# Attention and two MLPs on one core: conversions of weights moved behind a copy, and the last batch's scores, u and xT put in another order

## The chip, the core and the metric

One Trainium2 chip, one of its cores. The metric is the device time of one execution in microseconds (us), median of several executions; lower is better. The profile names the engines PE (matrix multiplies; PEld is its weight loads), DVE (vector), ACT (scalar), POOL and SP; SP issues most of the transfers (DMA).

## The reference

```python
def _attn_ref(q, k, v, phi):                       # all (4, 8, 576, ...), 32 memory slots
    a = softmax(phi, axis=2)                       # over the 32 slots of a token
    k_m = einsum('bhsm,bhsd->bhmd', a, k)          # 32 x 64 for each batch and head
    v_m = einsum('bhsm,bhsd->bhmd', a, v)
    attn = softmax(q @ k_m.T / 8, axis=-1)
    return attn @ v_m
x = attn_out as (2304, 512)
x = ((x @ w_a) * (x @ w_b)) @ w_out                # 512 -> 1536 -> 512
y = elu(x @ w_in) @ w_out2                         # 512 -> 2048 -> 512
```

As the kernel and its rows show it, phi's maximum and sum run over the 576 tokens of one slot (axis 2 of phi). q and k are drawn 200 times larger than v and phi.

## The kernel before

The weights come as 64-bit floats. A "unit" is one 128x512 block; it is loaded raw (512 KB, a POOL transfer) and turned into two float32r parts, high and low, by a fixed run of small steps on ACT (L113 magnitude, L119 low word, L133 the high part) and DVE (L155, L158, L142, L163, L168, L173, L176). `piece()` does the next step of the current unit, and `fill(n)` does n of them at the place where it is called. The step that begins a unit on DVE (L155) reads what ACT's L113 made for that unit.

All instructions are issued by hand: each engine runs its own instructions in the order in which the code calls them.

The first part of the kernel (to about 104 us) is the attention, one loop over the four batches i = 0 to 3. In iteration i, PE contracts a with k and v (`stage_kv`, L360), the means are turned (`stage_turn`, L380), PE makes the scores of batch i-1 (`stage_scores`, L401 and L405), and transposes a of batch i+1 (`stage_aT`, PE L336 and L338). ACT copies these transposes to SBUF (L340 and L343), which the next iteration's `stage_kv` reads. DVE makes the softmax of batch i-1 (`stage_softmax`: L427 maximum, L429 subtraction, ACT L431 exp) and, an iteration later, its sums and division (`stage_norm`: L445 to L451). `stage_xT` transposes the result on PE (L462, L466), rounds it into `xhi` on ACT (L69) and makes the rest `xlo` on DVE (L70).

attn @ v_m is never made. Instead u = v_m @ w is made for each 128 columns of w (`step_u`, PE L489, in two halves of 12 matmuls), rounded on ACT (L504), its rest made on DVE (L500), and spread by eight or sixteen small transfers into tiles `u` by batch (L513); the ab steps (`steps_ab`, PE L629) multiply u by xhi and xlo. The tile `ur`, in which u is rounded, has one buffer. For the first columns (f = 0), u is made for batches 0 and 1 in iteration 3 and for batches 2 and 3 behind the loop.

PSUM is held as two tiles of two banks (`pstile`, pool ps0) and four of one bank (`pone`, pool ps1); behind the attention ps1 is closed and its banks become two more of two banks (ps2). A step's deferred work (`defer`) runs in a later `step` or `tick`.

Order of the calls around the change, before:

```python
            stage_vT(i)
            if i:
                stage_scores(i - 1)
            fill(FILLS[i])
            if i + 1 < B:
                stage_aT(i + 1)
            if i:
                soft_tiles(i - 1)
                stage_softmax(i - 1)
```

Behind the loop: u of batches 2 and 3 (both halves), scores of batch 3, division and xT of batch 2, softmax and division of batch 3, then the ab steps of batches 0 and 1, u for the next columns, xT of batch 3, the ab steps of batch 2 and so on.

Of the kernel before, what the change touches and what calls it, by code (L numbers as in the profile page):

```python
# [7 lines left out]
F32 = mybir.dt.float32  # L8
# [5 lines left out]
AF = mybir.ActivationFunctionType  # L14
ALU = mybir.AluOpType
# [6 lines left out]
def attention_then_two_mlps(ctx, tc, q, kv, kv_left, phi, w_ab, w_o1, w_i2, w_o2, out):  # L22
# [13 lines left out]
    nc = tc.nc  # L36
    B, P, KC, S = q.shape
    M = 32
# [5 lines left out]
    SM = NJ * P  # L44
    LEFT = S - SM
# [15 lines left out]
    def pstile(name):  # L61
        turn[0] += 1
        return pss[turn[0] % len(pss)].tile([P, 2, 512], F32, tag="ps", name=name)

    def pone(name):
        return pstile(name)[:, 0] if len(pss) == 2 else ps1.tile([P, 512], F32, tag="one", name=name)

    def split_sb(hi, lo, src):
        nc.scalar.activation(out=hi, in_=src, func=AF.Copy)  # L69
        nc.vector.tensor_tensor(out=lo, in0=src, in1=hi.bitcast(F32), op=ALU.subtract)  # L70
# [117 lines left out]
    def drop(key):  # L188
        ready.pop(key)
        live[units[index[key]][1]] -= 1  # L190
# [3 lines left out]
    def fill(amount):  # L194
        credit[0] += amount
        while credit[0] >= 1.0:
            credit[0] -= 1.0
            if not piece():
                credit[0] = 0.0


    FILLS = 6, 6, 6, 6
# [35 lines left out]
    def tick():  # L238
        step(lambda: None, [], 0, "012")
# [11 lines left out]
    xhi = [pa.tile([P, 2, S], F32R, name=f"xhi{b}") for b in range(B)]  # L251
    xlo = [pa.tile([P, 2, S], F32R, name=f"xlo{b}") for b in range(B)]
# [75 lines left out]
    def stage_aT(b, us=(0, 1)):  # L328
        t = st["phi", b]
        if us[0] == 0:  # L330
            st["a", b] = p0.tile([P, 2, NJ + 1, P], F32, tag="a", name="a_t", bufs=1)
        a = st["a", b]
        tp, tl = pstile("tp_a"), pone("tl_a")
        for u in us:
            for j in range(NJ):
                nc.tensor.transpose(tp[:, u, j * P:(j + 1) * P], t[:, u, j * P:(j + 1) * P], ident)  # L336
        for u in us:
            nc.tensor.transpose(tl[0:LEFT, u * P:(u + 1) * P], t[:, u, SM:S], ident)  # L338
        c = slice(us[0], us[-1] + 1)
        nc.scalar.activation(  # L340
            out=a[:, c, 0:NJ, :].rearrange("p u j s -> p u (j s)"), in_=tp[:, c], func=AF.Copy
        )
        nc.scalar.activation(  # L343
            out=a[0:LEFT, c, NJ, :], in_=tl[0:LEFT, 0:2 * P].rearrange("p (u s) -> p u s", u=2)[:, c], func=AF.Copy
        )
        if us[-1] == 1:
            more_loads("phi")
# [46 lines left out]
    def stage_scores(b):  # L394
        qs = [st.pop(("q", b, u)) for u in range(2)]
        kt = kts[b % 2]
        sc, sl = pstile("sc"), pone("sl")
        for u in range(2):
            for j in range(NJ):
                for t in range(2):  # L400
                    nc.tensor.matmul(sc[:, u, j * P:(j + 1) * P], qs[u][:, t, j * P:(j + 1) * P],  # L401
                                     kt[:, u, t * P:(t + 1) * P], start=(t == 0), stop=(t == 1))
        for u in range(2):
            for t in range(2):
                nc.tensor.matmul(sl[0:LEFT, u * P:(u + 1) * P], qs[u][:, t, SM:S],  # L405
                                 kt[:, u, t * P:(t + 1) * P], start=(t == 0), stop=(t == 1))
        more_loads("q", "q")
        st["sc", b] = [
            (sc.rearrange("p u (g m) -> p u g m", m=M), P, 4 * NJ),
            (sl[0:LEFT, 0:2 * P].rearrange("p (u g m) -> p u g m", u=2, m=M), LEFT, 4),  # L410
        ]
# [38 lines left out]
            for o, m in both(at, n, sm):  # L450
                eng.tensor_tensor(out=o, in0=o, in1=m.to_broadcast(list(o.shape)), op=ALU.mult)  # L451

    def stage_xT(b):
        (at, _, _), (al, _, _) = st.pop(("at", b))
        tp, tl = pstile("tp_x"), pone("tl_x")

        def half(t, u):
            return t[u] if isinstance(t, list) else t[:, u]

        for u in range(2):  # L460
            for j in range(NJ):
                nc.tensor.transpose(tp[:, u, j * P:(j + 1) * P],  # L462
                                    half(at, u)[:, 4 * j:4 * j + 4, :].rearrange("p g m -> p (g m)"), st["ident"])
        split_sb(xhi[b][:, :, 0:SM], xlo[b][:, :, 0:SM], tp)
        for u in range(2):
            nc.tensor.transpose(tl[:, u * LEFT:(u + 1) * LEFT],  # L466
                                half(al, u)[0:LEFT].rearrange("p g m -> p (g m)"), st["ident"][0:LEFT, 0:LEFT])
        split_sb(xhi[b][:, :, SM:S], xlo[b][:, :, SM:S], tl[:, 0:2 * LEFT].rearrange("p (u s) -> p u s", u=2))

    u_t, g_t = {}, {}  # L470

    def step_u(f, amount, bs=tuple(range(B))):

        us = {b: pu.tile([P, 2, 2, 256], F32R, tag="u", name="u", bufs=5) for b in bs}
        ur = pu.tile([P, 2, KC, 2, 256], F32R, tag="ur", name="ur", bufs=1)
        u_t.update({(f, b): us[b] for b in bs})

        def half(k):  # L480
            ps = pstile("u_ps")

            def pe():
                whi, wlo = weights(("ab", f, k))
                for c in range(2):
                    for n, (v, w) in enumerate(((vthi, whi), (vthi, wlo), (vtlo, whi))):
                        for i in range(2):
                            r = slice(64 * i, 64 * i + 64)
                            nc.tensor.matmul(  # L489
                                ps[:, i, c * 256:c * 256 + 256], v[r, 2 * k + c].rearrange("p b m -> p (b m)"),  # L490
                                w[r, c * 256:c * 256 + 256], start=(n == 0), stop=(n == 2),
                            )
                if bs[-1] == B - 1:
                    drop(("ab", f, k))

            src = ps.rearrange("p i (c n) -> p i c n", c=2)
            hi, lo = [ur[:, :, 2 * k:2 * k + 2, x] for x in range(2)]

            def lower():
                nc.vector.tensor_tensor(out=lo, in0=src, in1=hi.bitcast(F32), op=ALU.subtract)  # L500
                if k == 1:
                    spread()

            step(pe, lambda: nc.scalar.activation(out=hi, in_=src, func=AF.Copy), amount / 2)  # L504
            defer(1, lower)

        def spread():
            for b in bs:
                for c in range(2):
                    for i in range(2):  # L510
                        o = 64 * c + M * i
                        src = ur[M * b:M * b + M, i].rearrange("p (k c) h n -> p k c (h n)", c=2)[:, :, c ^ (b % 2)]
                        nc.sync.dma_start(out=us[b][o:o + M].rearrange("p k h n -> p k (h n)").bitcast(F32),  # L513
                                          in_=src.bitcast(F32))

        half(0)
        half(1)

    with tc.manual_schedule():
        make_identity(nc, ident)  # L520
# [21 lines left out]
        for i in range(B):  # L542

            for n in (1, 0):
                for u in range(2):
                    stage_kv(i, n, u)
                stage_m(i, n)
            if i == 0:
                fill(4)
                a_max(1, 0)  # L550
                a_max(1, 1)
                a_exp(1, 0)
                a_exp(1, 1)
            if i > 1:
                stage_norm(i - 2, nc.vector)
            if i + 1 < B:
                a_end(i + 1, 0)
                a_end(i + 1, 1)
            if i == B - 1:
                step_u(0, 0, (0, 1))  # L560
            tick()
            if i > 1:
                stage_xT(i - 2)
            stage_turn(i, 1)
            stage_turn(i, 0)
            stage_kT(i)
            stage_vT(i)
            if i:
                stage_scores(i - 1)
            fill(FILLS[i])  # L570
            if i + 1 < B:
                stage_aT(i + 1)
            if i:
                soft_tiles(i - 1)
                stage_softmax(i - 1)
            if i + 2 < B:
                a_max(i + 2, 0)
                a_max(i + 2, 1)
                a_exp(i + 2, 0)
                a_exp(i + 2, 1)  # L580
        step_u(0, 0, (2, 3))
        tick()
        stage_scores(B - 1)
        stage_norm(B - 2, nc.vector)
        stage_xT(B - 2)


        last = B - 1
# [17 lines left out]
        st["at", last] = [(ats, *[rest[:, k, :, 0:4 * NJ] for k in range(2)]),  # L606
                          (als, *[rest[:, k, :, 4 * NJ:] for k in range(2)])]
        stage_softmax(last)
        tick()
        es_p.close()  # L610
        pss.append(ctx.enter_context(tc.tile_pool(name="ps2", bufs=2, space=PSUM, reuse_waits="tile")))
        stage_norm(last, nc.vector)
        tick()

        def steps_ab(f, b, amount):
            u = u_t.pop((f, b))
# [279 lines left out]
```

## Time and profile before

| | us |
|---|---|
| median of 3 runs (837.27 to 840.36) | 837.71 |
| the profiled execution | 838.2 |
| its span in the profile | 836.4 |
| PE busy in it | 794.7 (95%) |
| DVE busy | 610.3 (73%) |
| ACT busy | 413.6 (49%) |

The profile is one execution. The span is the time from its first to its last instruction; about 1.8 us of the execution's own time lie outside it. Shares of busy time are means over stages of different limits. PEclk is the share of TensorE's full clock that was granted.

### The profile page before, as it was taken

The numbers are of one execution on the slowest core, as the hardware profiler recorded it, in microseconds if no ns is written. First come the engines' busy times: TensorE is split into PE (matmuls) and PEld (weight loads), VectorE is DVE, ScalarE is ACT, GpSimd is POOL, SyncE is SP. The second block draws the span as 40 slices with busy tenths as digits, with TensorE's granted clock in tenths as the row PEclk, the third lists the DMA queues.
The fourth block names the chain that finished last, engine by engine and source line by source line (L and its number), as shares of the span: only waits on it lengthen the run. The fifth ranks groups of instructions, "written<-read, shape, count | busy, mean of one in ns | idle before, by whom it ended". The sixth has DMA issues, their size and how long they took to land.

```text
span 836.4 us, 13805 instructions
## 1 busy us (share of the span) xinstructions
PE 794.7 (95%) x5576; PEld 739.7 (88%) x5576; DVE 610.3 (73%) x1015; ACT 413.6 (49%) x636; POOL 43.1 (5%) x91
## 2 busy tenths in 40 slices
PE   4686799999999999999999999999999999999998
PEld 3575789999999999999999898889998889998896
DVE  4497877878887888567788852887777876776555
ACT  4354456655454444334358753566554565543360
POOL 3000000000000000000000000000000000000000
PEclk9598899999999999999999999999999999999999
DMA  9973267664775277516001200111111110100006
GB/s 302 367 252 91 61 161 178 159 152 109 176 175 125 80 177 177 125 30 150 26 1 51 74 27 1 53 49 52 50 51 51 51 51 25 51 26 1 1 1 226
DMA packets 32175, 82.95 MB, mean 99 GB/s; under 512 B 4848, under 2 KB 4848, under 8 KB 32112
## 3 DMA queue, kind: packets, MB, share of 16 engines
q1 hardware_dynamic: 22320, 46.41, 20.5%
q0 software_dynamic: 9792, 35.66, 14.4%
q8 instruction: 44, 0.72, 0.4%
q14 instruction: 19, 0.16, 0.1%
HBM read 52.17 MB, written 4.72 MB: 68 GB/s over the span
## 4 chain that ended last, share of the span: by engine, by line
PE 87%; DVE 4%; DMA 4%; ACT 2%; issue 1%; SPq 1%; POOL 1%; DVEq 0%; ACTq 0%; POOLq 0%
PE o_ps L796 24%; PE h_ps L753 24%; PE o_ps L671 17%; PE ab_ps L629 16%; DMA raw<-in_w_ab_dram 3%; PE u_ps L489 2%; PE sc L401 2%; PE pk L360 1%; DVE ur L500 1%; SPq L513 1%; DMA u<-ur 1%; DVE a_sb L638 0%; DVE at L429 0%; ACT gh L639 0%; DVE a L163 0%
## 5 line engine op out<-in xcount | busy, mean ns | idle before, releaser
L629 PE MATMUL ab_ps<-xhi,u 128*128 128x288 f32 x768 | 141.0, 301 | 5.3 <-DVE ur L500 2.6
L629 PEld LDWEIGHTS ab_ps<-xhi,u 128*128 128x128 f32 x768 | 116.1, 192 | 7.4 <-DVE ur L500 3.0
L796 PE MATMUL o_ps<-ulh,g2h 128*128 128x512 f32 x288 | 114.2, 397 | 0.0
L796 PE MATMUL o_ps<-ull,g2h 128*128 128x512 f32 x288 | 114.2, 396 | 0.0
L796 PE MATMUL o_ps<-ulh,g2l 128*128 128x512 f32 x288 | 103.5, 397 | 0.0
L771 DVE SCALAR_TENSOR_TENSOR e<-e,th 128x768 f32<-128x768 f32 x48 | 46.0, 959 | 76.5 <-ACT e L768 76.2
L753 PE MATMUL h_ps<-yh,usl 128*128 128x384 f32 x384 | 98.2, 336 | 0.0
L753 PE MATMUL h_ps<-yh,ush 128*128 128x384 f32 x384 | 98.1, 336 | 0.0
L753 PE MATMUL h_ps<-yl,ush 128*128 128x384 f32 x384 | 98.1, 336 | 0.0
L764 ACT ACTIVATE e<-h_ps 128x768 f32<-128x768 f32 x48 | 39.0, 812 | 96.1 <-PE h_ps L753 94.1
L629 PE MATMUL ab_ps<-xlo,u 128*128 128x288 f32 x384 | 83.3, 299 | 0.0
L671 PE MATMUL o_ps<-gh,ulh 128*128 128x288 f32 x384 | 83.0, 297 | 0.1
L671 PE MATMUL o_ps<-gh,ull 128*128 128x288 f32 x384 | 82.4, 296 | 0.0
L671 PE MATMUL o_ps<-gl,ulh 128*128 128x288 f32 x384 | 82.4, 295 | 0.0
L753 PEld LDWEIGHTS h_ps<-yh,ush 128*128 128x128 f32 x384 | 69.7, 188 | 1.3
L753 PEld LDWEIGHTS h_ps<-yh,usl 128*128 128x128 f32 x384 | 69.5, 188 | 0.0
L753 PEld LDWEIGHTS h_ps<-yl,ush 128*128 128x128 f32 x384 | 69.5, 188 | 0.0
L638 DVE TENSOR_TENSOR a_sb<-a_sb,ab_ps 128x576 f32<-128x576 f32 x48 | 36.1, 753 | 42.2 <-PE ab_ps L629 35.7
L796 PEld LDWEIGHTS o_ps<-ulh,g2l 128*128 128x128 f32 x288 | 54.2, 188 | 13.2
L796 PEld LDWEIGHTS o_ps<-ull,g2h 128*128 128x128 f32 x288 | 54.3, 188 | 12.5
L796 PEld LDWEIGHTS o_ps<-ulh,g2h 128*128 128x128 f32 x288 | 54.3, 188 | 12.5
L629 PEld LDWEIGHTS ab_ps<-xlo,u 128*128 128x128 f32 x384 | 63.0, 192 | 0.0
(115 smaller groups left out, 1385.2 us busy)
## 6 DMA issues: line engine op xcount, KB each, us to landing
u<-ur SPq DMA_DIRECT2D x192, 128.0 KB, 5.0
raw<-in_w_o_dram POOLq DMA_DIRECT2D x28, 512.0 KB, 4.1
raw<-in_w_ab_dram POOLq DMA_DIRECT2D x24, 512.0 KB, 5.6
kv_t<-in_kv_dram SPq DMA_DIRECT2D x16, 512.0 KB, 8.4
raw<-in_w_i_dram POOLq DMA_DIRECT2D x16, 512.0 KB, 3.7
q_t<-in_q_dram SPq DMA_DIRECT2D x8, 576.0 KB, 9.9
out_dram<-y SPq DMA_DIRECT2D x8, 512.0 KB, 2.9
phi_t<-in_phi_dram SPq DMA_DIRECT2D x3, 576.0 KB, 10.4
```

Source lines behind the costliest of these rows:

```text
L360: nc.tensor.matmul(pk[M * h:M * h + M, D * u:D * u + D], a[0:P if j < NJ else LEFT, u, j, M * h:M * h + M], rows, start=(j == 0), stop=(j ...
L401: nc.tensor.matmul(sc[:, u, j * P:(j + 1) * P], qs[u][:, t, j * P:(j + 1) * P], kt[:, u, t * P:(t + 1) * P], start=(t == 0), stop=(t == 1))
L489: nc.tensor.matmul(ps[:, i, c * 256:c * 256 + 256], v[r, 2 * k + c].rearrange("p b m -> p (b m)"), w[r, c * 256:c * 256 + 256], start=(n = ...
L500: nc.vector.tensor_tensor(out=lo, in0=src, in1=hi.bitcast(F32), op=ALU.subtract)
L513: nc.sync.dma_start(out=us[b][o:o + M].rearrange("p k h n -> p k (h n)").bitcast(F32), in_=src.bitcast(F32))
L629: nc.tensor.matmul(ps[:, h, 0:HS], u[:, kk, w, n * P:n * P + P], x[b][:, kk, h * HS:(h + 1) * HS], start=(kk == 0 and i == 0), stop=(kk == ...
L638: nc.vector.tensor_tensor(out=a_sb, in0=a_sb, in1=ps[:, :, 0:HS], op=ALU.mult)
L671: nc.tensor.matmul(ps[:, h, 0:HS], w[:, cc], g[:, h * HS:(h + 1) * HS], start=(n == 0 and i == 0), stop=(n == len(fs) - 1 and i == 2),)
L753: nc.tensor.matmul(ps[:, h, 0:HB], w[:, c], x[:, c, h * HB:(h + 1) * HB], start=(c == 0 and i == 0), stop=(c == KC - 1 and i == 2),)
L764: nc.scalar.activation(out=e, in_=ps[:, :, 0:HB], func=AF.Relu, scale=-1.0)
L771: nc.vector.scalar_tensor_tensor(out=e, in0=e, scalar=1.0, in1=th, op0=ALU.add, op1=ALU.mult)
L796: nc.tensor.matmul(ps[:, k, :], g[:, c * P:(c + 1) * P], w, start=(f == fs[0] and i == 0), stop=(f == fs[-1] and i == 2),)
```

## The change

Four edits. (1) In the loop, `fill` moves behind `stage_aT`, so that ACT's steps of the conversion are called behind its copies of the transposed a. (2) Behind the loop the scores of batch 3 come first; u of batches 2 and 3 is made in halves, the first half behind these scores, the second behind the softmax of batch 3 and behind the change of PSUM pools. (3) `step_u` rounds and subtracts only the partitions of its own batches (64 of 128 where it has two batches). (4) xT of batch 2 is held in three one-bank tiles instead of one of two banks and one of one; its rounding and subtraction are done by half, and the subtraction is called behind the softmax of batch 3.

```diff
-    def stage_xT(b):
+    def stage_xT(b, single=False):
         (at, _, _), (al, _, _) = st.pop(("at", b))
-        tp, tl = pstile("tp_x"), pone("tl_x")
+        if single:
+            tps, tl = [pone("tp_x") for _ in range(2)], pone("tl_x")
+        else:
+            tp, tl = pstile("tp_x"), pone("tl_x")
+            tps = [tp[:, u] for u in range(2)]
...
-        split_sb(xhi[b][:, :, 0:SM], xlo[b][:, :, 0:SM], tp)
...
-        split_sb(xhi[b][:, :, SM:S], xlo[b][:, :, SM:S], tl[:, 0:2 * LEFT].rearrange("p (u s) -> p u s", u=2))
+        parts = [(slice(SM, S), slice(0, 2), tl[:, 0:2 * LEFT].rearrange("p (u s) -> p u s", u=2))]
+        if single:
+            parts = [(slice(0, SM), u, tps[u]) for u in range(2)] + parts
+        else:
+            parts = [(slice(0, SM), slice(0, 2), tp)] + parts
+
+        def upper(c, u, src):
+            nc.scalar.activation(out=xhi[b][:, u, c], in_=src, func=AF.Copy)
+
+        def lower(c, u, src):
+            nc.vector.tensor_tensor(out=xlo[b][:, u, c], in0=src, in1=xhi[b][:, u, c].bitcast(F32), op=ALU.subtract)
+
+        if not single:
+            for p in parts:
+                upper(*p)
+                lower(*p)
+            return None
+        for p in parts:
+            upper(*p)
+        return lambda: [lower(*p) for p in parts]
...
-    def step_u(f, amount, bs=tuple(range(B))):
+    def halves_u(f, amount, bs=tuple(range(B))):
...
-            src = ps.rearrange("p i (c n) -> p i c n", c=2)
-            hi, lo = [ur[:, :, 2 * k:2 * k + 2, x] for x in range(2)]
+            r = slice(M * bs[0], M * bs[-1] + M)
+            src = ps[r].rearrange("p i (c n) -> p i c n", c=2)
+            hi, lo = [ur[r, :, 2 * k:2 * k + 2, x] for x in range(2)]
...
-        half(0)
-        half(1)
+        return [lambda: half(0), lambda: half(1)]
+
+    def step_u(f, amount, bs=tuple(range(B))):
+        for half in halves_u(f, amount, bs):
+            half()
...
             if i:
                 stage_scores(i - 1)
-            fill(FILLS[i])
             if i + 1 < B:
                 stage_aT(i + 1)
+            fill(FILLS[i])
...
-        step_u(0, 0, (2, 3))
+        stage_scores(B - 1)
+        halves = halves_u(0, 0, (2, 3))
+        halves[0]()
+        stage_norm(B - 2, nc.vector)
         tick()
-        stage_scores(B - 1)
-        stage_norm(B - 2, nc.vector)
-        stage_xT(B - 2)
+        lower_x = stage_xT(B - 2, True)
...
         stage_softmax(last)
-        tick()
+        lower_x()
         es_p.close()
         pss.append(ctx.enter_context(tc.tile_pool(name="ps2", bufs=2, space=PSUM, reuse_waits="tile")))
+        halves[1]()
+        tick()
         stage_norm(last, nc.vector)
-        tick()
```

## Rows read from the trace of the kernel before

**Rows 1.** Windows: stretch, its us, busy us (instructions) by engine, clock, DMA share, GB/s.
```profile
80.00:86.00 6.00, 6.00 (x40) 5.88 (x40) 4.39 (x9) 0.00 (x0) 0.00 (x0) 0.73 0.57 131
...
104.00:146.00 42.00, 39.67 (x288) 38.02 (x288) 32.52 (x57) 24.27 (x56) 3.22 (x6) 0.96 0.72 167
146.00:836.00 690.00, 686.05 (x4224) 643.01 (x4224) 507.67 (x818) 343.85 (x490) 30.29 (x55) 1.00 0.28 78
```
**Rows 2.** Timeline, iteration 0: start, us, instruction, [engine idle before, who ended it].
```profile
20.80 0.66 PE L336 MATMUL tp_a<-ident,phi_t 128*128 128x128 f32 x4 [0.16 <-DVE phi_t L321]
...
24.50 0.65 ACT L119 ACTIVATE lw<-raw 128x512 bf16<-128x512 uint32 x1 [2.29 <-DMA raw<-in_w_ab_dram]
25.06 1.00 ACT L340 ACTIVATE a_t<-tp_a 128x1024 f32<-128x1024 f32 x1
...
26.12 1.08 PE L360 MATMUL pk<-kv_t,a_t 128*32 128x64 f32 x32 [4.44 <-ACT a_t L340]
...
34.16 0.37 PE L360 MATMUL pk<-kv_t,a_t 128*32 128x64 f32 x2 [2.82 <-issue]
```
**Rows 3.** DMA queues between 31 and 35 us: packets, MB, share.
```profile
q8 instruction: 1, 0.02, 2.0%
```
**Rows 4.** Timeline, iteration 1 and the begin of 2.
```profile
37.07 0.68 ACT L113 ACTIVATE a<-raw 128x512 f32<-128x512 f32 x1
...
38.50 0.42 DVE L155 TENSOR_SCALAR a<-a 128x512 f32<-128x512 f32 x1
...
41.41 1.22 DVE L427 TENSOR_REDUCE smx<-sc 128x32 f32<-128x1024 f32 x1 [0.83 <-PE sc L401]
...
43.51 1.02 ACT L340 ACTIVATE a_t<-tp_a 128x1024 f32<-128x1024 f32 x1 [4.26 <-PE tp_a L336]
...
44.43 0.36 ACT L343 ACTIVATE a_t<-tl_a 64x256 f32<-64x256 f32 x1
...
49.39 1.06 PE L462 MATMUL tp_x<-ident,at 128*128 128x128 f32 x8 [1.42 <-DVE at L451]
```
**Rows 5.** Timeline, iterations 2 and 3.
```profile
54.61 0.42 DVE L155 TENSOR_SCALAR a<-a 128x512 f32<-128x512 f32 x1
...
56.01 1.22 DVE L427 TENSOR_REDUCE smx<-sc 128x32 f32<-128x1024 f32 x1
...
57.45 1.02 ACT L340 ACTIVATE a_t<-tp_a 128x1024 f32<-128x1024 f32 x1 [2.09 <-PE tp_a L336]
...
65.20 1.09 PE L462 MATMUL tp_x<-ident,at 128*128 128x128 f32 x8 [1.66 <-DVE ur L500]
```
**Rows 6.** Timeline behind the loop.
```profile
74.57 1.36 ACT L431 ACTIVATE at<-at 128x1024 f32<-128x1024 f32 x2 [2.65 <-DVE at L429]
...
77.46 1.94 ACT L504 ACTIVATE ur<-u_ps 128x1024 fp32r<-128x1024 f32 x2 [1.52 <-DMA u<-ur]
...
79.79 5.44 PE L401 MATMUL sc<-kt,q_t 128*128 128x128 f32 x32 [4.13 <-DVE ur L500]
80.79 1.53 DVE L445 TENSOR_REDUCE ssm<-at 128x32 f32<-128x1024 f32 x2
...
82.96 1.50 DVE L451 TENSOR_TENSOR at<-at,ssm 128x1024 f32<-128x1024 f32 x2
...
88.37 1.23 DVE L70 TENSOR_TENSOR xlo<-tp_x,xhi 128x1024 fp32r<-128x1024 f32 x1 [3.91 <-ACT xhi L69]
...
93.01 1.26 DVE L445 TENSOR_REDUCE small<-at 128x16 f32<-128x512 f32 x2
...
103.72 0.85 PE L629 MATMUL ab_ps<-xhi,u 128*128 128x288 f32 x2 [2.61 <-DVE ur L500]
```
**Rows 7.** Windows of u's matmuls alone (columns as in Rows 1, POOL left out).
```profile
72.00:74.00 2.00, 0.98 (x12) 0.78 (x12) 0.00 (x0) 0.00 (x0) 1.00 0.87 294
```
**Rows 8.** The tile ur: its spreading transfers, 66 to 135 us.
```profile
L513 SPq DMA_DIRECT2D u<-ur x39: 585/595/1621, 66.3 to 134.4; - x39
...
DMA to landing us min/median/max: 2.3/4.0/6.5
```

More of the change, by code (lines that the diff above doesn't have):

```diff
@@ L461, in stage_xT @@
             for j in range(NJ):
-                nc.tensor.transpose(tp[:, u, j * P:(j + 1) * P],
+                nc.tensor.transpose(tps[u][:, j * P:(j + 1) * P],
                                     half(at, u)[:, 4 * j:4 * j + 4, :].rearrange("p g m -> p (g m)"), st["ident"])
-        split_sb(xhi[b][:, :, 0:SM], xlo[b][:, :, 0:SM], tp)
         for u in range(2):
```

## The prediction

> **What bounds the kernel now.** I read the windows first, then the timeline of the first 112 us with the waits that it names. In the windows PE is busy 686.05 us of the 690 behind 146 us, and 39.67 of 42 between 104 and 146 [rows 1]: from about 104 us on PE is the bound, and all that the change touches lies before. So the question is only by how much the ab step that begins at 103.72 us [rows 6] moves; from there the shift is carried to the end one for one. Before 104 us no engine is full: PE waits for others, and these waits are the reader's to see in the timeline. In iteration 0 it waits 4.44 us for ACT's copy of the transposed a, then 2.82 us for nothing that the profile shows [rows 2]. In iterations 2 and 3 it waits 1.42 and 1.66 us for DVE [rows 4, 5]: there DVE's softmax chain sets the pace. Behind the loop it waits 4.13 us because u's rounding waits for transfers out of the same buffer, and 2.61 us for DVE again [rows 6].
>
> **Edit 1, iteration 0: a gain.** The transposes of a for batch 1 end at 20.80 + 0.66 = 21.46. ACT's copy starts only at 25.06, since the conversion step L119 stands ahead of it and waits for its raw weights until 24.50; that a ready copy stays behind it shows that ACT keeps its order [rows 2]. With the copy called first it starts at 21.5, 3.56 us earlier, and so do PE's matmuls at 26.12. Term: -3.6.
>
> **Edit 1, iteration 1: a loss.** Here the same exchange works the other way. ACT's copy of a waits for PE (4.26 us, until 43.51), since PE transposes a behind the scores. In the kernel before, the conversion step L113 ran in that idle time, at 37.07, and DVE's L155, which reads it, at 38.50. Now L113 stands behind both copies, which end at 44.43 + 0.36 = 44.79, and ends 0.68 later, at 45.47. DVE's L155 waits for it, and behind L155 on DVE, in the order of the calls, stand the rest of the conversion and then the softmax of batch 0. From the start of L155 to the end of the conversion DVE took 41.41 - 0.83 - 38.50 = 2.08 us, so the softmax starts at 47.55 in place of 41.41: 6.1 us later, against 3.6 won. PE's xT at 49.39 waited for the end of this chain on DVE (1.42 us), so it has no slack [rows 4]. Net at xT of batch 0: +2.6. Nobody else uses the wait: ACT's exps hang on the same softmax.
>
> **The clock.** PE's work before that xT ends at 49.39 - 1.42 = 47.97; it moves up by 3.6 while xT moves back by 2.6, so PE idles 7.6 us. In the trace an idle time of 4.13 us ahead of 79.79 left the matmuls behind it at the lower level: the mean of 0.73 from 80 to 86 us is 0.5 until 83.2 [rows 1, 6]. So I take the same here: 3.4 us at 1.2 in place of 2.4 GHz, worth 1.7 us. Bounds: nothing if the level holds, 3.4 if it comes back as much later again. Term: +1.7.
>
> **Edit 1, iteration 2: the same loss again.** The copy at 57.45 and its second part take 1.28 as above, then two conversion steps of about 0.65 each stand on ACT ahead of what L155 needs (by L119's 0.65 [rows 2] and L113's 0.68 [rows 4]), so L155 starts at 60.0 in place of 54.61. From L155 to the softmax DVE takes 56.01 - 54.61 = 1.40: softmax at 61.4 in place of 56.01, +5.4 [rows 5]. In iteration 3 division, u's subtraction and then PE's xT at 65.20 follow on DVE without slack (PE waits 1.66 for it), and since PE's work before it moves by 4.3 only (2.6 + 1.7) and xT by 9.7, PE idles there up to 1.66 + 5.4 us, less what u's second half waits for its PSUM tile: +1.7 for the clock once more. Iteration 3 has no copy of a, so there the move is worth nothing. Sum of edit 1 at the scores of batch 2: -3.6 + 6.1 + 1.7 + 5.4 + 1.7 = +11.4 (rounded terms +11.3).
>
> **Edits 2 to 4, behind the loop: a gain.** I work in the old times and let the +11.4 stand aside. The scores of batch 3 fill PE at once, and the wait of 4.13 us goes. The first half of u follows; its rounding would find the eight transfers landed (they let it go at 77.46, and PE reaches the end of that half at about 78, an estimate: 72 [rows 7], some 5 for the scores [rows 6] and 1 for the half). DVE sets the pace: exp of batch 2 ends at 74.57 + 1.36 = 75.9; division takes 82.96 + 1.50 - 80.79 = 3.7, to 79.6; u's subtraction 1.2, as the 128x1024 of 88.37, to 80.8; softmax of batch 3 and xT's subtraction together 93.01 - 88.37 = 4.64 in either order, to 85.5 (halving adds one instruction to each engine, some 0.1) [rows 6]. The new pools' banks are held until then, so PE's second half of u starts at 85.5. It takes 0.98 at the upper level [rows 7], 1.9 at the lower, which I take, since PE has idled some 5 us; rounding is half of 1.94 and the subtraction 1.2: 89.6. Only then does the division of batch 3 start on DVE, which it did at 93.01: -3.4. A new wait can eat of it. The spreading of batches 2 and 3 moves from behind 80.8 to behind 89.6. Eight issues of 0.6 and a landing of 4.0 (2.3 to 6.5) end at 98.1 (96.4 to 100.6) [rows 8]; the rounding of u for the next columns overwrites the buffer, ACT's later work stands behind it, and it must start by 103.72 - 1.0 - 1.2 - 3.4 = 98.1. So 0 to 2.5 is lost; I take 0.4, and the term is -3.0 (-3.4 to -0.9).
>
> **Edit 3.** No row has 64 partitions of 1024 elements. From above the 128x1024 instructions bound it (about 1.0 on ACT, 1.2 on DVE [rows 6]), from below the 64x256 copy of 0.36 [rows 4]. I take the same as before, being equal in length along a partition; the bound is -1.3 for the two on the path. Whether rounding 64 other partitions of the one buffer still waits for the eight transfers no row shows; by the times above it costs nothing either way.
>
> **The 2.82 us stall.** It stands in PE's stream inside one block of equal matmuls, while one packet of the instruction queue moves [rows 2, 3], so I read it as PE waiting for its own program, and let it move along with the work. The Trainium skill ("Runtime: NRT & Kernel Launch", Instruction fetch mechanics) has it that an engine's program is streamed in blocks by its own queue and that the cost of a block's edge is mostly hidden; the row differs, and by that rule the stall would go and the sum would be 2.8 lower. The sum keeps it; the other end of its price is nothing.
>
> **Sum.** 11.4 - 3.0 = +8.4 us. Against the profiled execution's 838.2 that is 846.6; its median is 0.5 lower, so 846.1 against 837.71. A measurement tells some 0.5% (4.2 us) from no change, so this is slower.
>
> **Rivals.** *A: faster.* The conversions do not hold DVE, and the gains stand alone: -3.6 and -3.4 give 830.7. It decides at one place: if L155 of iteration 1 starts before ACT's copy of a ends. For it speaks only the 4.44 us wait that the move does remove; against it, ACT's order in [rows 2] and DVE's order L155, then softmax, in [rows 4]. Chance 0.08. *B: about the same.* The losses shrink: the level holds at both restarts (-3.4), the stall goes (-2.8), the short partitions pay (-1.3): +0.9, 838.6. PE's waits between 104 and 146 us, 2.3 in all [rows 1], may swallow part too. For it: each is a bound above; against: they must come together. Chance 0.10. *C: slower still.* The start of iteration 1 gains nothing, as its next tiles are not there yet or the stall grows by as much (+3.6), and the spreading lands late (+2.1): 851.8. Chance 0.08. *D: the rounding of fewer partitions does not do what it is written for;* by the above it changes no time here, so it has no chance of its own. The forecast keeps 0.74.
>
> **The numbers.** The likeliest is 846.1, by itself 842 to 851. To leave out no more than 2 in 10 (A, most of C, the tails) I take 839.5 to 851. Faster 0.08 (A); same, 833.5 to 841.9, 0.10 (B); slower 0.82.
>
> **What would show it.** In the changed profile: ACT's L340 copy in iteration 0 at about 21.5; in iterations 1 and 2 DVE idle some 5 us ahead of L155, ended by ACT's L113, and the softmax behind it; PE idle 5 to 8 us ahead of both xT with a clock of 0.5 behind; no wait of u's rounding for transfers at the scores of batch 3; the division of batch 3 some 5 us behind the xlo of batch 2; the first ab step of batch 2 near 112. The forecast is wrong if DVE does not wait for L113, or if the clock stays up in both gaps and the stall at 31 us is gone.

## The result and the profile after

The changed kernel takes 846.25 us (median of 11 runs), the kernel before 839.6 us in the same session: ratio 1.0077, 95% interval [1.0056, 1.0098]. It is slower, by 4.7 to 8.2 us. The forecast was 846.1 against 837.71, a step of +8.4; by the ratio the step is +6.5.

In the file of the changed kernel the lines behind the loop have other numbers: xT is L467, its upper part L479 and lower part L482, u's matmuls are L512, its subtraction L524, its rounding L528, the ab steps L658. First the window of the long stage, with the columns of [rows 1]:

```profile
154.00:840.00 686.00, 685.86 (x4229) 643.19 (x4228) 506.70 (x817) 343.93 (x489) 30.65 (x55) 1.00 0.28 77
```

Behind 154 us PE is busy 685.86 of 686, as it was before [rows 1]; all of the difference lies ahead of that. Then the timeline of the changed kernel (start, duration, engine, line, tile, and in brackets the idle time ahead and what ended it), first the loop, then what is behind it:

```profile
start us, us, engine line op out<-in xcount [idle before <-releaser]
22.75 1.02 ACT L340 ACTIVATE a_t<-tp_a 128x1024 f32<-128x1024 f32 x1 [1.82 <-PE tp_a L336]
23.83 1.08 PE L360 MATMUL pk<-kv_t,a_t 128*32 128x64 f32 x32 [0.75 <-ACT a_t L340]
...
30.22 0.37 PE L360 MATMUL pk<-kv_t,a_t 128*32 128x64 f32 x2 [1.18 <-issue]
...
40.32 1.02 ACT L340 ACTIVATE a_t<-tp_a 128x1024 f32<-128x1024 f32 x1 [6.97 <-PE tp_a L336]
41.51 0.67 ACT L113 ACTIVATE a<-raw 128x512 f32<-128x512 f32 x1
42.20 0.43 DVE L155 TENSOR_SCALAR a<-a 128x512 f32<-128x512 f32 x1 [7.47 <-ACT a L113]
44.21 1.22 DVE L427 TENSOR_REDUCE smx<-sc 128x32 f32<-128x1024 f32 x1
...
52.19 1.94 PE L467 MATMUL tp_x<-ident,at 128*128 128x128 f32 x8 [7.40 <-DVE at L451]
...
60.11 1.09 PE L405 MATMUL sl<-kt,q_t 128*64 128x128 f32 x8
...
64.77 0.43 DVE L155 TENSOR_SCALAR a<-a 128x512 f32<-128x512 f32 x1 [6.26 <-ACT a L113]
66.18 1.22 DVE L427 TENSOR_REDUCE smx<-sc 128x32 f32<-128x1024 f32 x1
...
74.66 1.97 PE L467 MATMUL tp_x<-ident,at 128*128 128x128 f32 x8 [4.98 <-DVE ur L524]
...
83.28 1.09 PE L405 MATMUL sl<-kt,q_t 128*64 128x128 f32 x8
83.38 1.23 DVE L427 TENSOR_REDUCE smx<-sc 128x32 f32<-128x1024 f32 x1 [0.74 <-PE sc L401]
...
84.29 3.84 PE L401 MATMUL sc<-kt,q_t 128*128 128x128 f32 x32
90.14 1.02 ACT L528 ACTIVATE ur<-u_ps 64x1024 fp32r<-64x1024 f32 x1 [2.88 <-PE u_ps L512]
...
97.27 0.58 PE L512 MATMUL u_ps<-ush,vthi 64*128 64x256 f32 x2 [5.52 <-DVE xlo L482]
...
100.01 1.23 DVE L524 TENSOR_TENSOR ur<-u_ps,ur 64x1024 fp32r<-64x1024 f32 x1 [2.80 <-ACT ur L528]
...
101.27 1.28 DVE L445 TENSOR_REDUCE small<-at 128x16 f32<-128x512 f32 x2
...
108.40 1.01 ACT L528 ACTIVATE ur<-u_ps 128x1024 fp32r<-128x1024 f32 x1
...
112.13 0.85 PE L658 MATMUL ab_ps<-xhi,u 128*128 128x288 f32 x2 [2.60 <-DVE ur L524]
```

Read it by the differences to the rows of before. In iteration 0 the matmuls behind ACT's copy start at 23.83 against 26.12, and the stall "issue" is 1.18 in place of 2.82 [rows 2]. In iteration 1 DVE idles 7.47 us ahead of L155, ended by ACT's L113, which stands behind the copy; the softmax starts at 44.21 against 41.41 and xT at 52.19 against 49.39, +2.8 [rows 4]. In iteration 2 the same row comes back with 6.26 us: softmax at 66.18 against 56.01, xT of batch 1 at 74.66 against 65.20, +9.46 [rows 5]. The softmax of batch 2 starts at 83.38 against 72.06, +11.3. Behind the loop the last scores follow at once and the rounding at 90.14 waits for no transfer; the division of batch 3 begins at 101.27 against 93.01, and the ab step at 112.13 against 103.72, +8.4 [rows 6]. The span grew by 8.1. The ends of the scores of batches 1 and 2, and the softmax of batch 2, in the kernel before:

```profile
55.24 1.09 PE L405 MATMUL sl<-kt,q_t 128*64 128x128 f32 x8
...
71.08 1.09 PE L405 MATMUL sl<-kt,q_t 128*64 128x128 f32 x8
...
72.06 1.22 DVE L427 TENSOR_REDUCE smx<-sc 128x32 f32<-128x1024 f32 x1
```

### The profile page after: what moved, and what is told of

Same layout as the page of the kernel before. It is cut to its first block, busy times and chain, and to the rows that moved or that the text cites. A ratio compares the mean times of both kernels' runs of the same rounds, so it can differ in the third digit from the quotient of the medians.

```text
span 844.5 us, 13807 instructions
## 1 busy us (share of the span) xinstructions
PE 800.5 (95%) x5576; PEld 744.9 (88%) x5576; DVE 610.9 (72%) x1016; ACT 414.1 (49%) x637; POOL 43.4 (5%) x91
## 4 chain that ended last, share of the span: by engine, by line
PE 90%; DVE 5%; DMA 3%; ACT 2%; issue 0%; SPq 0%; ACTq 0%; DVEq 0%
PE o_ps L825 24%; PE h_ps L782 24%; PE o_ps L700 18%; PE ab_ps L658 18%; PE sc L401 2%; DMA phi_t<-in_phi_dram 2%; PE u_ps L512 2%; DVE ur L524 1%; PE pt L380 1%; DVE at L429 0%; PE sl L405 0%; PE tp_x L467 0%; PE pk L360 0%; DMA raw<-in_w_ab_dram 0%; DVE at L451 0%
## 5 line engine op out<-in xcount | busy, mean ns | idle before, releaser
L658 PE MATMUL ab_ps<-xhi,u 128*128 128x288 f32 x768 | 141.2, 301 | 2.7 <-DVE ur L524 2.6
L658 PEld LDWEIGHTS ab_ps<-xhi,u 128*128 128x128 f32 x768 | 116.5, 193 | 4.4 <-DVE ur L524 3.0
L658 PE MATMUL ab_ps<-xlo,u 128*128 128x288 f32 x384 | 83.6, 300 | 0.0
L658 PEld LDWEIGHTS ab_ps<-xlo,u 128*128 128x128 f32 x384 | 63.3, 193 | 0.0
## 6 DMA issues: line engine op xcount, KB each, us to landing
q_t<-in_q_dram SPq DMA_DIRECT2D x8, 576.0 KB, 12.2
```

Of the source, the lines that this page charges most:

```text
L658: nc.tensor.matmul(ps[:, h, 0:HS], u[:, kk, w, n * P:n * P + P], x[b][:, kk, h * HS:(h + 1) * HS], start=(kk == 0 and i == 0), stop=(kk == ...
```

## The experiments

Each was timed in five rounds against the kernel before; differences in us are the ratio times 838. "Before" is 837.89 for the first four; 837.79 for the late iterations one at a time and for the division of batch 3, the last one; 838.74 for the other four. Kernels of different sessions are compared by their ratios to "before".

**Edit 1 alone** (kernel before, one line moved):

```
-            fill(FILLS[i])
             if i + 1 < B:
                 stage_aT(i + 1)
+            fill(FILLS[i])
```

> Only edit 1: the call of the conversion steps stands behind the copy of the transposed a, the rest is the kernel before. My theory (the loss is edit 1's alone: in iterations 1 and 2 the conversion steps start only behind ACT's copy, and DVE's L155 holds the softmax): 9 to 12 us slower than before, about 848 to 851 against 839; DVE idle 5 to 8 us ahead of L155 of iterations 1 and 2, the softmax of batch 1 some 10 us later than its 56.01. Rival 1 (edit 1 is neutral and the new order behind the loop costs the time): within 2 us of before. Rival 2 (the conversions hold nobody, so that the gain of iteration 0 stays): 3 to 4 us faster.

845.41 us, ratio 1.009 [1.0076, 1.0104]: +7.5. The direction is mine, the size is not. In its timeline L155 and the softmaxes stand as in the changed kernel (softmax of batch 1 at 65.92, of batch 2 at 83.19), so 11 us are lost by then. But the old order behind the loop gives some 3 of them back (1.6 of wait and 1.6 of clock):

```profile
86.98 1.91 ACT L504 ACTIVATE ur<-u_ps 128x1024 fp32r<-128x1024 f32 x2
89.29 3.84 PE L401 MATMUL sc<-kt,q_t 128*128 128x128 f32 x32 [2.49 <-DVE ur L500]
...
111.63 0.85 PE L629 MATMUL ab_ps<-xhi,u 128*128 128x288 f32 x2 [2.61 <-DVE ur L500]
```

u's rounding starts without the 1.52 us wait for transfers, PE waits 2.49 in place of 4.13, and the scores take 3.84 us in place of 5.44 [rows 6], at the upper level. Coming later, batch 3 finds the transfers landed.

**Edits 2 to 4 alone** (the changed kernel, with the conversion steps put back ahead of the copy):

```
+            fill(FILLS[i])
             if i + 1 < B:
                 stage_aT(i + 1)
-            fill(FILLS[i])
```

> Only edits 2 to 4: the new order behind the loop, with the halves of u and the narrower rounding, and the conversion steps where the kernel before has them. My theory: 3 us faster than before (2 to 4), the wait of 4.13 us ahead of the last scores gone, and a first ab step of batches 0 to 2 about 3 us ahead of 103.72. Rival 1 (the new order is what costs): 5 us or more slower. Rival 2 (the spreading of batches 2 and 3, now issued later, becomes the wait and eats all of it): within 1 us of before.

833.55 us, ratio 0.9953 [0.9935, 0.9971]: -3.9, as expected. PE's wait of 4.13 us ahead of the last scores is gone; the next one on PE is for DVE's softmax and xlo ahead of the second half of u. ACT's rounding of u still waits for transfers, against my reading that they would have landed, but DVE is at the division until 79.97 and needs it no earlier:

```profile
72.70 3.84 PE L401 MATMUL sc<-kt,q_t 128*128 128x128 f32 x32
...
78.87 1.02 ACT L528 ACTIVATE ur<-u_ps 64x1024 fp32r<-64x1024 f32 x1 [2.33 <-DMA u<-ur]
...
86.05 0.58 PE L512 MATMUL u_ps<-ush,vthi 64*128 64x256 f32 x2 [5.03 <-DVE xlo L482]
```

The two parts do not add: 7.5 - 3.9 is 3.6, the change is +6.5. On top of edit 1, edits 2 to 4 bring 1.1 us (1.0077 against 1.009), which the intervals do not tell from nothing: what they take away, edit 1 had taken away already.

**Edit 1 in iteration 0 alone** (kernel before):

```
-            fill(FILLS[i])
+            if i:
+                fill(FILLS[i])
             if i + 1 < B:
                 stage_aT(i + 1)
+            if not i:
+                fill(FILLS[i])
```

> The kernel before with the conversion steps behind the copy of a in iteration 0 alone; in iterations 1 to 3 they stand where they stood. My theory: the 2.3 to 3.6 us that the copy starts earlier reach the end, 2 to 4 us faster. Rival (iteration 1 has slack for them to vanish in: its softmax waits for something that does not move): within 1 us of before, the softmax of batch 0 still near 41.4.

837.5 us, ratio 0.999 [0.9975, 1.0006]: a miss; at most 2 us are won. Its profiled execution was one of its fastest runs (834.37), and there the head start lasts: xT of batch 0 comes 5.2 us earlier than before (49.39 [rows 4]) and the ab step 3.4 (103.72 [rows 6]). What the slower executions lose of it no trace shows; a new wait is seen in this one, since DVE's L308 needs phi of batch 3.

```profile
39.35 1.41 DVE L308 TENSOR_REDUCE nm<-phi_t 128x1 f32<-128x576 f32 x2 [0.70 <-DMA phi_t<-in_phi_dram]
...
44.16 1.06 PE L462 MATMUL tp_x<-ident,at 128*128 128x128 f32 x8 [2.26 <-DVE at L451]
...
100.29 0.69 PE L632 MATMUL ab_ps<-xhi,u 128*128 128x288 f32 x2 [2.61 <-DVE ur L500]
```

**Edit 3 alone** (kernel before, u rounded on the 64 partitions of its batches):

```
-            src = ps.rearrange("p i (c n) -> p i c n", c=2)
-            hi, lo = [ur[:, :, 2 * k:2 * k + 2, x] for x in range(2)]
+            r = slice(M * bs[0], M * bs[-1] + M)
+            src = ps[r].rearrange("p i (c n) -> p i c n", c=2)
+            hi, lo = [ur[r, :, 2 * k:2 * k + 2, x] for x in range(2)]
```

> The kernel before with edit 3 alone: u is rounded on the 64 partitions of its own batches, nothing is moved. Theory 1 (the rounding writes a part of the same buffer and still waits for every transfer out of it): no change, within 1 us, the rounding of batches 2 and 3 near 77.46 still ended by a transfer and PE's 4.13 us wait ahead of the last scores still there. Theory 2 (the narrower rounding waits only for transfers out of its own partitions, of which there are none): its wait of 1.52 us goes and the kernel is 1 to 2 us faster.

838.69 us, ratio 1.0006 [0.9992, 1.002]. Theory 1: half the partitions take the same time (two in 1.93 us, 1.94 before [rows 6]), and the wait for transfers out of the other half of the buffer stays.

```profile
77.44 1.93 ACT L505 ACTIVATE ur<-u_ps 64x1024 fp32r<-64x1024 f32 x2 [1.32 <-DMA u<-ur]
```

**Edits 2 to 4 with edit 1 in iteration 0 alone** (edit of the third experiment, made in the changed kernel).

> Edits 2 to 4 as in the changed kernel, and edit 1 in iteration 0 alone. My theory (the losses of edit 1 in iterations 1 and 2 are avoided, and the two gains are earned in different places): the 4.3 us of edits 2 to 4 and 0.4 to 3.5 of iteration 0, so 5 to 8 us faster than before. Rival (what iteration 0 wins is gone by the tail, since more of it hangs on transfers that do not move): 4 us faster, as edits 2 to 4 alone.

832.29 us, ratio 0.9918 [0.9898, 0.9938]: -6.9, as expected, and the fastest version here. So edits 2 to 4 are worth 3.9 us on the kernel before, 6.0 on the third experiment, 1.1 on edit 1; and iteration 0 is worth 0.8 on the kernel before, which is not told from nothing, and 2.9 on edits 2 to 4 (the intervals just touch). Phi's wait is there too (1.69 us).

**The late iterations one at a time** (the same kernel; the second has `i in (1, 3)` and `i in (0, 2)` in place of `i > 1` and `i <= 1`):

```
-            if i:
+            if i > 1:
                 fill(FILLS[i])
             if i + 1 < B:
                 stage_aT(i + 1)
-            if not i:
+            if i <= 1:
                 fill(FILLS[i])
```

> Edits 2 to 4, and edit 1 in iterations 0 and 1 alone; in iteration 2 the conversion steps stand where they stood. My theory (each late iteration costs by itself: 6.1 for iteration 1 and 1.7 for the clock behind it): 5 to 8 us slower than edits 2 to 4 with edit 1 in iteration 0 alone, so within 2 us of before. Rival 1 (only the first delay counts, the second hides in it): as slow as the changed kernel, 5 to 8 slower than before. Rival 2 (the delay of iteration 1 is made up in iteration 2, whose transfers and weights are ready earlier): 4 or more faster than before.

> Edits 2 to 4, and edit 1 in iterations 0 and 2 alone; in iteration 1 the conversion steps stand where they stood. My theory (5.4 for iteration 2 and 1.7 for the clock behind it): 5 to 7 us slower than edits 2 to 4 with edit 1 in iteration 0 alone, so within 2 us of before, the softmax of batch 1 some 5 us behind the end of its scores. Rival 1 (iteration 2 alone has slack, as its conversions are due later): 4 or more faster than before. Rival 2 (iteration 2 carries nearly all of the loss): 4 or more slower than before.

838.17 us, ratio 1.0004 [0.9988, 1.0021], and 839.1 us, ratio 1.0009 [0.9991, 1.0026]: against 0.9918 the move costs 7.2 us in iteration 1 and 7.6 in iteration 2. Both have a price of their own, and in each trace L155 waits in its own iteration alone:

```profile
41.51 0.43 DVE L155 TENSOR_SCALAR a<-a 128x512 f32<-128x512 f32 x1 [7.32 <-ACT a L113]
...
57.74 0.42 DVE L155 TENSOR_SCALAR a<-a 128x512 f32<-128x512 f32 x1
```

(the first of the two kernels; the second:)

```profile
35.09 0.42 DVE L155 TENSOR_SCALAR a<-a 128x512 f32<-128x512 f32 x1
...
60.54 0.43 DVE L155 TENSOR_SCALAR a<-a 128x512 f32<-128x512 f32 x1 [6.54 <-ACT a L113]
```

**The conversion steps behind the softmax** (changed kernel):

```
             if i + 1 < B:
                 stage_aT(i + 1)
-            fill(FILLS[i])
             if i:
                 soft_tiles(i - 1)
                 stage_softmax(i - 1)
+            fill(FILLS[i])
```

> The changed kernel with one line moved: in every iteration the conversion steps are called behind the softmax, not ahead of it. My theory (the changed kernel loses because L155 stands ahead of the softmax on DVE, and for nothing else): the loss goes and the gains stay, 3 to 7 us faster than before; the softmax of batch 1 near 52 to 56, not 66.18. Rival 1 (the conversions themselves are then too late for u or for ACT's later work): 2 us or more slower than before. Rival 2 (the loss lies in ACT's queue, not in DVE's order): as the changed kernel, 5 to 9 slower.

844.76 us, ratio 1.007 [1.005, 1.009]: my theory fell as I had put it. The softmax no longer waits for L155, and nothing is won:

```profile
39.88 1.22 DVE L427 TENSOR_REDUCE smx<-sc 128x32 f32<-128x1024 f32 x1 [4.85 <-PE sc L401]
...
45.13 0.43 DVE L155 TENSOR_SCALAR a<-a 128x512 f32<-128x512 f32 x1 [0.92 <-ACT a L113]
...
51.95 1.30 PE L467 MATMUL tp_x<-ident,at 128*128 128x128 f32 x5 [5.49 <-DVE at L451]
```

The softmax starts at 39.88, as soon as the scores are there, but xT comes 12.1 us later, against 8.0 before (41.41 to 49.39 [rows 4]): the conversions now run between softmax and division, 4.1 us of DVE (43.07 to 47.14) with a wait of 0.92 in them. And DVE's 4.85 us of idle time ahead of the scores' end stays empty. So I now read the loss in this way: DVE's conversions must lie where DVE waits for PE's scores. Ahead of the copy they do; on either side of the softmax they stand in the chain that PE waits for.

**PE kept busy in the two gaps** (changed kernel; the extra transposes of the identity are written over by the real ones):

```
+        for _ in range({0: 40, 1: 28}.get(b, 0)):
+            nc.tensor.transpose(tl[:, 0:P], st["ident"], st["ident"])
         for u in range(2):
             for j in range(NJ):
```

> The changed kernel with 40 more transposes of the identity ahead of xT of batch 0 and 28 ahead of xT of batch 1, into a bank that the real ones write later: PE then works in the gaps of 7.40 and 4.98 us in which it idled; nothing else is altered. My theory (the lower granted clock behind these gaps costs 1.7 us each, 1.9 and 2.5 in the changed kernel's trace): xT takes 1.06 in place of 1.94, the clock behind stays at the upper level, and the kernel is 3 to 4.5 us faster than the changed one, so 2 to 5 slower than before. Rival 1 (what PE wins is given back to the next wait for DVE): less than 1 us faster than the changed one. Rival 2 (the clock falls there whatever PE does): xT still 1.94, no change.

844.54 us, ratio 1.0068 [1.0048, 1.0088]: by the ratios 0.8 us less than the changed kernel, not told from nothing.

```profile
45.99 4.58 PE L466 MATMUL tl_x<-ident 128*128 128x128 f32 x40
53.39 1.09 PE L469 MATMUL tp_x<-ident,at 128*128 128x128 f32 x8 [2.81 <-DVE at L451]
...
107.59 1.02 ACT L530 ACTIVATE ur<-u_ps 128x1024 fp32r<-128x1024 f32 x1 [0.76 <-PE tp_x L469]
```

xT does take 1.09 in place of 1.94 us, so the clock obeys what PE did ahead of it. But only the second gap pays. Behind the first, the mean clock from 46 to 57 us is 0.89 in place of 0.53, but the level falls a little later and the scores take 4.67 us where 3.84 are possible; from xT to the end of batch 1's scores 8.5 us pass in place of 9.0. Behind the second it is 7.0 in place of 9.7. Behind the loop 1.1 are given back (28.8 us from the end of batch 2's scores to the ab step, 27.8 in the changed kernel), 0.76 of it where u's rounding for the next columns, which in the changed kernel starts without idle time, now waits. In the profiled execution 1.8 us of span are left of it.

**PE kept busy in the gap behind the loop** (edits 2 to 4 with edit 1 in iteration 0 alone, and 40 matmuls ahead of the second half of u):

```
+        for _ in range(40):
+            nc.tensor.matmul(tl[:, 2 * P:4 * P], xhi[0][:, 0, 0:P], xhi[0][:, 0, P:3 * P], start=True, stop=True)
         return lambda: [lower(*p) for p in parts]
```

> Edits 2 to 4 with edit 1 in iteration 0 alone, and 40 matmuls into an unused part of a bank in the gap of some 5 us ahead of the second half of u of batches 2 and 3. Theory 1 (the lower clock behind that gap costs all that it stretches, 0.75 us on the half of u and 1.7 on the ab steps behind): 1.5 to 2.5 us faster than the same kernel without them. Theory 2 (from the second half of u on DVE sets the pace, so only what comes ahead of it counts): 0.5 to 1 faster. Rival (the clock falls nevertheless): no change.

834.6 us, ratio 0.9947 [0.9928, 0.9966], where the same kernel without them has 0.9918 in the same session: it is 2.4 us slower than that, if anything (the intervals just overlap), which neither theory has; the rival has the reason nearly right. The windows, first without and then with the 40 matmuls:

```profile
78.00:98.00 20.00, 13.11 (x102) 11.97 (x99) 16.96 (x34) 10.04 (x17) 0.69 (x1) 0.83 0.32 79
...
108.00:134.00 26.00, 24.03 (x187) 23.04 (x187) 23.63 (x43) 18.65 (x43) 2.17 (x4) 1.00 0.63 164
```

```profile
78.00:98.00 20.00, 16.09 (x137) 14.94 (x138) 16.61 (x34) 9.87 (x16) 0.69 (x1) 1.00 0.32 80
...
108.00:134.00 26.00, 22.93 (x163) 22.27 (x163) 21.60 (x39) 16.70 (x41) 2.11 (x4) 0.87 0.60 153
```

From 78 to 98 us the granted clock of 0.83 becomes 1.00, and from 108 to 134 us 1.00 becomes 0.87: the lower level is met later. The traces show two things that I had not allowed for (the first row without the 40 matmuls, then three with them):

```profile
119.05 0.39 PE L512 MATMUL u_ps<-ush,vthi 64*128 64x256 f32 x2 [1.11 <-ACT y L711]
```

```profile
83.08 0.29 DVE L482 TENSOR_TENSOR xlo<-tl_x,xhi 128x128 fp32r<-128x128 f32 x1 [1.03 <-PE tl_x L492]
...
116.52 0.66 ACT L119 ACTIVATE lw<-raw 128x512 bf16<-128x512 uint32 x1 [2.01 <-DMA raw<-in_w_ab_dram]
...
117.89 0.58 PE L514 MATMUL u_ps<-ush,vthi 64*128 64x256 f32 x2 [2.35 <-ACT y L713]
```

The 40 matmuls (L492) write the tile that holds the last part of xT, and DVE's subtraction out of that tile now waits 1.03 us for them. From the sums of batch 2 (74.06 without, 72.51 with) to the ab step (98.71, 97.62) 25.11 us pass in place of 24.65, so the gap was not filled without cost. Behind the ab step PE then waits 2.35 us in place of 1.11 for ACT, whose L119 waits 2.01 us for raw weights (0.77 without), and right behind this longer wait the clock is at the lower level (0.50 from 118 to 122 us). So this experiment does not isolate what the clock behind that gap is worth.

**The division of batch 3 ahead of u's second subtraction** (edits 2 to 4 with edit 1 in iteration 0 alone):

```
         halves[1]()
-        tick()
         stage_norm(last, nc.vector)
+        tick()
```

> Edits 2 to 4 with edit 1 in iteration 0 alone, and behind the loop the division of batch 3 called ahead of u's second subtraction of batches 2 and 3 (the changed kernel has it behind). Theory 1 (DVE idles 2.8 us ahead of that subtraction, and the division fills it): 1 to 2.5 us faster than the same kernel without. Theory 2 (the subtraction and the eight transfers behind it then start 1 to 2 us later, and u's rounding for the next columns waits for the last of them): 0 to 2 us slower, with a transfer named as what that rounding waits for.

836.96 us, ratio 0.9988 [0.9972, 1.0004], against 0.9918: theory 2, by the ratios at some 6 us, three times what I had allowed. The two traces differ by 5.3 us of span; 1.2 of it stand already ahead of the exchange (the sums of batch 2 begin at 75.29 against 74.06), and 3.1 come from there to the ab step (27.76 us in place of 24.65).

```profile
88.91 1.23 DVE L524 TENSOR_TENSOR ur<-u_ps,ur 64x1024 fp32r<-64x1024 f32 x1
...
99.48 1.02 ACT L528 ACTIVATE ur<-u_ps 128x1024 fp32r<-128x1024 f32 x1 [4.51 <-DMA u<-ur]
...
103.05 0.85 PE L661 MATMUL ab_ps<-xhi,u 128*128 128x288 f32 x2 [5.38 <-DVE ur L524]
```

DVE's idle time is filled, but the subtraction starts 1.1 us later than ACT's rounding allows (86.78 + 1.02 = 87.80), and the transfers leave that much later. They also land later. In the DMA view (tile, queue, count, KB each, median us from issue to landing), of 86 to 98 us without the exchange, then of 88 to 100 us with it:

```profile
u<-ur SPq DMA_DIRECT2D x8, 128.0 KB, 2.3
```

```profile
u<-ur SPq DMA_DIRECT2D x8, 128.0 KB, 4.7
```

Without the exchange the next weight load (512 KB) is issued at 93.55, behind all eight (87.85 to 92.92); with it at 92.02, between the third and the fourth. The first three then land in 2.3 us, the rest in 4.7 to 5.1. That the load is the reason is read from this order, not tested: in the trace of the experiment before this one transfers behind a load at 103.08 land in 4.7 to 5.6 too, but in the trace of the first busy gaps some land in 3.4 to 4.1 with no load just ahead of them.

## Why the prediction was right, point by point

**The bound.** PE sets the end behind 154 us; the ab step moved by 8.4, the span by 8.1.

**Iteration 0, -3.6.** The matmuls moved by 2.3 only, since phi and the transposes were later, and the shorter stall gave 1.6 more: the start of the scores is 3.8 ahead (32.56 against 36.40). The sum had kept the stall at 2.82. So that 3.2 us are left at the next copy (40.32 against 43.51), near the term, is in part luck. Whether the stall is an edge between two blocks of PE's program no run shows. The Trainium skill ("Runtime: NRT & Kernel Launch", Instruction fetch mechanics) would have such an edge mostly hidden. The stall is 1.18 here and 0.75 in the third experiment, so neither that rule nor the fixed price fits.

**Iterations 1 and 2.** Net +2.6 forecast at xT of batch 0, +2.8 measured; +9.7 and +9.5 at xT of batch 1; +11.4 and +11.3 at the softmax of batch 2. The one-at-a-time experiments give 7.2 and 7.6 us where the terms, with the clock's 1.7 in each, say 7.8 and 7.1. Rival A had its test in L155 of iteration 1: it starts at 42.20, behind both copies (40.32 on), and the rival is out. The reason I gave, DVE's order of L155 and softmax, was half of it (the experiment with the softmax first).

**The clock, 1.7 twice.** xT at the lower level is there (1.94 against 1.06, 1.97 against 1.09), and the first busy-gap experiment shows that PE's idle time brings it. The term was mis-sized twice. From xT to the end of the scores behind it PE takes 9.0 and 9.7 us in place of 6.9 and 7.0, so 2.1 and 2.7; DVE's chain took up the excess, for the +12.2 at the end of batch 2's scores are +11.3 at the softmax behind it. And with the gaps filled, only 0.8 of the 3.4 us came back in the median, 1.8 in the profiled span.

**Behind the loop, -3.0.** From the softmax of batch 2 to the ab step it was 31.66 us and is 28.75: -2.9. Nothing was lost to the spreading, as its transfers landed in 2.3 us where the sum had taken 4.0; the division experiment shows the loss to be close. Rival D is true and costs nothing, as costed.

**What failed.** "I work in the old times and let the +11.4 stand aside": taken alone, edit 1 costs 7.5 and not 11.4, for in the old order the wait of 4.13 us and the lower clock shrink by 3.2 us when batch 3 comes later; and edits 2 to 4 then have little left to take away: from the softmax of batch 2 to the ab step 28.44 us pass with edit 1 alone (83.19 to 111.63) and 28.75 with all edits. The two errors cancel in the sum, since it followed the path of the kernel with all edits. The step in the medians, +6.5, is 1.9 below the forecast and 1.6 below the step of the spans. Most of this lies in the base: the profiled execution of the kernel before took 838.2 us and the forecast started from 837.71, the median of three runs, while the median of eleven is 839.6. So it is in part luck that the forecast time of 846.1 meets 846.25 so closely.

## What to carry to other kernels

Before moving work on one engine, ask which idle time of another engine it was filling: the wait that the move removes was paid for in one iteration, the idle time that it leaves empty was used in two others. Work may move in the one iteration where its data are late and stay elsewhere; that alone turned +6.5 into -6.9 us. Edits that shorten the same wait do not add, so price each on the kernel with the others in place.

## What the runs showed of the hardware

An ACT or DVE instruction on 64 partitions of 1024 elements took as long as on 128: 1.02 and 1.23 us. PE's stall "issue" inside equal matmuls stands at the same place in iteration 0 of all thirteen kernels; it took 2.82 to 2.89 us in the three that keep the old iteration 0, and 0.75 to 2.50 us in the ten with edit 1 there. Work put into PE's idle time raised the granted clock from 0.83 to 1.00 (78 to 98 us), and the lower level came later instead, behind a wait that had grown from 1.11 to 2.35 us. Transfers of 128 KB landed in 2.3 us (median of eight) by themselves and in 4.7 to 5.1 behind a load of 512 KB.
